# Two more units summed by the vector engine, and four squares of every sixteen on another queue

## The chip, the cores and the metric

The kernel runs on one core of a Trainium2 chip. A core has five engines that run their own instruction streams in order and wait for each other by semaphores: PE (TensorE, matmuls; PEld is its weight load), DVE (VectorE), ACT (ScalarE), POOL (GpSimd) and SP (SyncE, which here only issues DMAs). The metric is the device time in microseconds of one execution. Before the change it is 930.43 us, the median of three runs (929.61 to 931.49).

## The reference

Eight batches of twelve heads go through softmax attention with a soft cap on the scores; the result, 448 tokens by 768 channels per batch, goes through a mixing layer. Shapes: q, k, v are 8 x 12 x 448 x 64, all in fp32.

```python
scores = scale * np.matmul(q, k.transpose(0, 1, 3, 2))
scores = cap * np.tanh(scores / cap)
attn = np.exp(scores - max)                      # max over the last axis
x = (attn / (sum(attn) + 1e-9)) @ v              # then heads side by side: 448 x 768
theta = x @ w_theta
y = w_tok_r @ (x * np.cos(theta)) + w_tok_i @ (x * np.sin(theta))
u = x + y
out = u + np.maximum(u @ w_ch, 0.0)
```

## The kernel before

**Units and slots.** Two heads make a unit, so a batch has six units and the kernel 48. The main loop (L519) runs over slots s. Slot s computes the scores of unit s in two halves (A and B, L216; one PSUM tile holds a half, so B waits for the tanh of A) and the products of unit s-1 with v (V, L260). ACT does tanh (tA, tB, L221) and exp (eA, eB, L227), and copies the product out of PSUM (cV).

**Row sums.** The sum of the exponentials over the keys is taken on PE with a matrix of ones (R, L280). Units 0 to 9 (`DIRECT = 10`) are summed straight from the exponentials: units 0 to 5 two at a time, units 6 to 9 each by itself. From unit 10 on DVE first adds the four key blocks up into `ps` (aA, one addition, L249; aB, two, L252), and PE sums only `ps`, for a pair of units at once. I inverts the sums of a pair, spreads them by DMA into `bc`, and N (L315) multiplies x with them, two units at a time.

**The mixing layer.** Batch b's layer runs in the six slots after its attention, beside the next batch's attention. T is theta (18 matmuls for each of the six channel blocks), y two ACT steps out of PSUM, d three DVE steps of range reduction (L362 to L364), sc the cosine and sine of a pair of channel blocks on ACT (L369, L370), r the products with x (L374) and f a transpose of 32 x 32 squares (L378). D (`carry`, L380) then moves the squares of a pair of blocks to their places by 16 DMAs of 56 KB (L388). h and l split the result into high and low parts (ACT L393, DVE L399), M multiplies with the token weights (L408 to L410), m adds to x (L413), u splits u, C is the channel product (L334 to L336), c its output (L420), X the split of the next batch's x. P splits q and k of a coming unit on DVE (L192, L193; from unit 14 on).

**Weights.** Weights come as raw words and are split on the chip, one block at a time (`WEIGHTS`; `>` loads, `*` scales on ACT at L110, `#` scales on DVE at L113, a bare name does the rest). The splitting of th, tk and ch blocks fills the first eight slots and is finished in slots 8, 11, 12 and 13. The high part of a block is a copy, on DVE (L125), or on ACT (L123) where the block says so: ch3, ch4 and ch5.

**What sets the order.** No scheduler reorders anything: each engine gets its instructions in the order in which the scripts name them. `FRONT` stands for slots 0 to 7, `PARTS` for the six slots of each later batch, `OTHER` for slots that differ, such as (0, 0) and (0, 1), which are slots 8 and 9. A word's instructions stand behind all earlier words' on their engine, DMAs on the queue that issues them.

Of the kernel before, what the change touches and what calls it, by code (L numbers as in the profile page):

```python
# [19 lines left out]
P = 128  # L20
# [5 lines left out]

FIRST = 8

DIRECT = 10

FILL = {"before the branch": 8, "first scores": 2, "half": 8, "slot": 10}

# [4 lines left out]
def softcap_attn_then_spectral_mix(ctx, tc, qk2, v, cap, w_theta, w_tok, w_ch, outT):  # L37
    nc = tc.nc
    B, NP, P, _, S = qk2.shape
# [14 lines left out]
    w_theta, w_ch = (w.bitcast(I32).rearrange("m p j (n two) -> m p j n two", two=2) for w in (w_theta, w_ch))  # L54
# [16 lines left out]
    wch_h = const.tile([P, NJ, DM], F32R, name="wch_h")  # L71
    wch_l = const.tile([P, NJ, DM], F32R, name="wch_l")
# [56 lines left out]
    def room_g(at):  # L129
        def room():  # L130
            st = g_sb[:, at : at + 3 * DM]
            raw = st[:, : 2 * DM].rearrange("p (j n two) -> p j n two", j=NJ, two=2)
            return raw, st[:, 2 * DM :].rearrange("p (j n) -> p j n", j=NJ)
        return room

    def room_t(i, name):
        def room():
            raw = g_sb[:, (12 + 2 * i) * S : (14 + 2 * i) * S]
            t = wk.tile([P, S], F32, tag="zl", name=f"{name}_t", bufs=2)
            return raw.rearrange("p (n two) -> p n two", two=2), t  # L140
        return room

    steps = {}

    def weight_steps():
        for m in range(NJ):
            ms = slice(m * P, (m + 1) * P)
            steps["th", m] = Split(room_g((0, 6 * S)[m % 2]), w_theta[m], wth_h[:, :, ms], wth_l[:, :, ms])
            steps["ch", m] = Split(room_g((0, 6 * S, 8 * S, 0, 8 * S, 0)[m]), w_ch[m], wch_h[:, :, ms], wch_l[:, :, ms], m > 2)
        for c in range(NC2):  # L150
            steps["tk", c] = Split(room_t(c % 2, f"swk{c}"), w_tok[c], wtk_h[:, c], wtk_l[:, c])


    WEIGHTS = {
# [86 lines left out]
    def add_half(k, half):  # L241

        if k < DIRECT and not state["general"]:
            return
# [37 lines left out]
    def sums(k, halves=(0, 1)):  # L282

        alone = state["general"] or NP <= k < DIRECT
        if not alone and k % 2 == 0:
# [94 lines left out]
    def carry(b, i):  # L380

        at = 4 * S * i
        to = 4 * S * (i - 1) if i else 12 * S
        z, t = (g_sb[:, n : n + 4 * S].rearrange("p (c m d) -> p c m d", m=4, d=32) for n in (at, to))
        for m in range(4):
            for d in range(4):
                queue = nc.gpsimd if b == B - 1 and i and d % 2 else nc.sync
                queue.dma_start(t[32 * m : 32 * m + 32, :, d, :], z[32 * d : 32 * d + 32, :, m, :])  # L388

    def z_high(b, j, h):  # L390
# [27 lines left out]
    def chan_out(b, m):  # L418
# [4 lines left out]
    FRONT = "A tA w0 eA Va R0 B tB Vb cV v R1 q w1 n I eB aA aB w2 x"  # L423
    PARTS = (
# [8 lines left out]
    )  # L433
    OTHER = {
        (0, 0): "A tA eA V cV w0 v R I B tB eB aA aB q T0 y0 d0 w1 T1 y1 d1 sc0 w2 T2 y2 r0 r1 f0 f1 d2 D0",
        (0, 1): "A tA eA V cV N v R I B tB eB aA aB q T3 y3 d3 sc1 T4 r2 r3 f2 f3 D1 y4 d4 T5 y5 d5",
        (B - 2, 4): "V cV u3 u4 u5 R I C0 c0 C1 X0 X1 c1 C2 X2 X3 c2",
        (B - 2, 5): "N X4 X5 T0+ y0+ d0+ T1+ y1+ d1+ sc0+ T2+ r0+ r1+ f0+ f1+ D0+ y2+ d2+ T3+ y3+ d3+ sc1+ T4+ r2+ r3+ f2+ f3+ D1+ y4+ d4+"
                    " T5+ y5+ d5+ sc2+ C3 c3 r4+ h0a+ l0a+ h0b+ l0b+ r5+ f4+ f5+ D2+ C4 c4 h1a+ C5 c5",
# [4 lines left out]
    def pipeline(general):  # L444
# [6 lines left out]
        def run(s, b, word):  # L451
# [33 lines left out]
            elif word == "I":  # L485
                if done:
                    invert(k)
            elif word == "q":
                if s + 2 <= WHOLE:
                    load_qk(s + 2)  # L490
            elif word == "P":
                if WHOLE <= s + 1 < NS:
                    prep(s + 1)
            elif name == "w":
                weights(s, "abc"[i])
            elif word == "N":
                norm(s - 3)
                norm(s - 2)
            elif word == "n":
                for n in {4: (0, 1), 5: (2, 3), 7: (4, 5)}.get(s, ()):  # L500
                    norm(n)
            elif word == "x":
                for j in {5: range(2), 6: range(2, 4), 7: range(4, NJ)}.get(s, ()):
                    split_x(0, j, "xs")
            elif name == "u":
                split_x(b, i, "us")
            elif name == "X":
                if b + 1 < B:
                    split_x(b + 1, i, "xs")
            elif name in ("h", "l", "M"):  # L510
                {"h": z_high, "l": z_low, "M": mix}[name](b, i, half)
            else:
                {"T": theta, "y": turns, "d": reduce, "sc": sincos, "r": rotate, "f": flip, "D": carry, "m": mix_out, "C": chan,
                 "c": chan_out}[name](b, i)
# [12 lines left out]

    load_consts()
    weight_steps()
    load_qk(0)  # L530
    first = (("th", 0), ("th", 1))
# [46 lines left out]
```

## Time and profile before

| | |
|---|---|
| median of three runs | 930.43 us |
| profiled execution: its time, its span | 927.67 us, 925.9 us |
| PE busy | 912.4 us (99%) |
| DVE busy | 653.0 us (71%) |
| ACT busy | 613.8 us (66%) |
| POOL busy | 10.8 us (1%) |
| share of PE, ACT, DVE in the chain that ended last | 80%, 11%, 5% |
| granted clock of PE | full in all 40 slices |

Busy is the time in which an engine has an instruction running; the span goes from the first instruction to the last. The profiled execution lies below the three timed runs, so differences are to be taken from its own time and then set against the median. Slots differ in length: slot 8 runs from about 75.9 to 96.7 us, slot 9 from 96.7 to 117.6, and from slot 14 on a batch takes about 110 us.

### The profile page before, as it was taken

To read this page: it belongs to the slowest core of one execution; us is meant where nothing else is said; L and a number is where in the kernel's file an instruction comes from. 1 tells how busy PE (TensorE), PEld (TensorE's weight loads), DVE (VectorE), ACT (ScalarE), POOL (GpSimd) and SP (SyncE) were. 2 spreads that over 40 slices of the span, in tenths; PEclk is the share of its full clock that TensorE was granted. 3 is DMA by queue.
4 is the path that set the end of the run, shared out by engine and by line. 5 is a ranking of instruction groups with operands and counts; after the bars stand their busy time and mean duration, and the time that the engine had idled before them with its cause. 6 is when DMAs were issued, how large, how long until landed. Compare 5 with 4: busy or idle time off the path is not lost.

```text
span 925.9 us, 12930 instructions
## 1 busy us (share of the span) xinstructions
PE 912.4 (99%) x4912; PEld 661.1 (71%) x4912; DVE 653.0 (71%) x967; ACT 613.8 (66%) x639; POOL 10.8 (1%) x22
## 2 busy tenths in 40 slices
PE   8999999999999999999999999999999999999997
PEld 4334666578767777787687677867877777789986
DVE  5998766987865588656977568665786558865741
ACT  7997875568855697646975579646885569753420
POOL 0000000000000000000000000000000000000310
PEclk9999999999999999999999999999999999999999
DMA  6764155432533244232552226422253333411611
GB/s 231 241 202 137 27 120 151 138 98 58 120 75 107 83 82 94 72 113 60 100 126 75 70 63 123 95 80 85 58 120 77 101 89 79 77 41 38 113 36 62
DMA packets 201863, 90.67 MB, mean 98 GB/s; under 512 B 175296, under 2 KB 187584, under 8 KB 201792
## 3 DMA queue, kind: packets, MB, share of 16 engines
q1 hardware_dynamic: 201280, 88.84, 37.8%
q0 software_dynamic: 512, 0.92, 0.5%
q8 instruction: 40, 0.66, 0.3%
q14 instruction: 31, 0.25, 0.1%
HBM read 45.68 MB, written 11.01 MB: 61 GB/s over the span
## 4 chain that ended last, share of the span: by engine, by line
PE 80%; ACT 11%; DVE 5%; issue 1%; DMA 1%; SPq 1%; DVEq 0%; ACTq 0%
PE s L216 11%; PE a L260 11%; PE mx L410 7%; PE mx L408 7%; PE mx L409 7%; PE ch L334 6%; PE ch L336 6%; PE ch L335 6%; PE th L334 5%; PE th L335 5%; PE th L336 5%; ACT p L221 4%; PE r L280 4%; ACT L221 2%; ACT p L227 1%
## 5 line engine op out<-in xcount | busy, mean ns | idle before, releaser
L221 ACT ACTIVATE p<-s,qscale 112x1792 f32<-112x1792 f32 x96 | 168.5, 1755 | 118.9 <-PE s L216 117.1
L227 ACT ACTIVATE p<-p,cap_sb 112x1792 f32<-112x1792 f32 x96 | 170.3, 1787 | 0.3
L260 PE MATMUL a<-p,v 112*64 112x448 f32 x768 | 156.5, 546 | 0.0
L260 PEld LDWEIGHTS a<-p,v 112*64 112x64 f32 x768 | 50.2, 136 | 88.2 <-issue 77.0
L334 PE MATMUL th<-xs,wth_h 128*128 128x448 f32 x288 | 107.0, 372 | 0.0
L334 PE MATMUL ch<-us,wch_h 128*128 128x448 f32 x288 | 106.9, 371 | 0.0
L335 PE MATMUL ch<-us,wch_h 128*128 128x448 f32 x288 | 105.5, 366 | 0.0
L335 PE MATMUL th<-xs,wth_h 128*128 128x448 f32 x288 | 105.5, 366 | 0.0
L336 PE MATMUL ch<-us,wch_l 128*128 128x448 f32 x288 | 105.5, 366 | 0.0
L336 PE MATMUL th<-xs,wth_l 128*128 128x448 f32 x288 | 105.4, 366 | 0.0
L252 DVE TENSOR_TENSOR ps<-ps,p 112x896 f32<-112x896 f32 x76 | 82.8, 1089 | 2.2
L410 PE MATMUL mx<-wtk_h,zl_False 128*128 128x448 f32 x192 | 70.6, 367 | 1.9 <-DVE zl_False L399 1.3
L408 PE MATMUL mx<-wtk_h,zh_False 128*128 128x448 f32 x192 | 71.4, 372 | 0.0
L420 DVE SCALAR_TENSOR_TENSOR x<-ch,x 128x448 f32<-128x448 f32 x48 | 29.8, 622 | 58.6 <-PE ch L336 58.6
L409 PE MATMUL mx<-wtk_l,zh_False 128*128 128x448 f32 x192 | 70.1, 365 | 0.0
L374 DVE TENSOR_TENSOR g_sb<-g_sb,x 128x896 f32<-128x896 f32 x48 | 50.8, 1086 | 19.0 <-ACT g_sb L370 19.0
L362 DVE SCALAR_TENSOR_TENSOR g_sb<-g_sb 128x448 f32<-128x448 f32 x48 | 29.5, 615 | 46.7 <-ACT g_sb L357 46.7
L334 PEld LDWEIGHTS ch<-us,wch_h 128*128 128x128 f32 x288 | 54.1, 188 | 9.6 <-issue 4.6
L334 PEld LDWEIGHTS th<-xs,wth_h 128*128 128x128 f32 x288 | 54.1, 188 | 9.6 <-issue 4.5
L336 PEld LDWEIGHTS ch<-us,wch_l 128*128 128x128 f32 x288 | 54.1, 188 | 4.8 <-DVE wch_l L127 0.2
L335 PEld LDWEIGHTS ch<-us,wch_h 128*128 128x128 f32 x288 | 54.2, 188 | 4.6 <-DVE us L326 0.3
L335 PEld LDWEIGHTS th<-xs,wth_h 128*128 128x128 f32 x288 | 54.2, 188 | 4.6 <-DVE xs L326 0.3
(82 smaller groups left out, 1567.1 us busy)
## 6 DMA issues: line engine op xcount, KB each, us to landing
g_sb<-g_sb SPq DMA_DIRECT2D x368, 56.0 KB, 2.0
qk_sb<-in_qk SPq DMA_DIRECT2D x35, 448.0 KB, 3.6
v<-in_v SPq DMA_DIRECT2D x48, 224.0 KB, 2.8
bc<-ri SPq DMA_DIRECT2D x96, 112.0 KB, 2.3
out_dram<-x SPq DMA_DIRECT2D x48, 224.0 KB, 1.9
qk<-in_qk SPq DMA_DIRECT2D x13, 448.0 KB, 3.8
g_sb<-in_wth SPq DMA_DIRECT2D x6, 768.0 KB, 5.5
g_sb<-in_wch SPq DMA_DIRECT2D x6, 768.0 KB, 5.8
```

The source lines that it names most:

```text
L216: nc.tensor.matmul(sp[:CP, i, hh, :S], kk[k][rows, 1, ks], qq[k][rows, 0, :], start=n == 0, stop=n == len(products) - 1)
L221: nc.scalar.activation(pt[k, half], spt.pop((k, half))[:CP, :, :, :S], AF.Tanh, scale=qscale[:CP])
L227: nc.scalar.activation(pp, pp, AF.Exp, scale=cap_sb[:CP])
L252: nc.vector.tensor_tensor(pst[k], pst[k], pt[k, 1][:, i], op=ALU.add)
L260: nc.tensor.matmul(acc[hh * D : (hh + 1) * D, :S], va[:, hh, c, :], pt[k, c // 2][:, c % 2, hh, :], start=c == 0, stop=c == NCH - 1)
L334: nc.tensor.matmul(acc[:, :S], wh[:, j, ms], t[:, 0, :], start=j == 0, stop=False)
L335: nc.tensor.matmul(acc[:, :S], wh[:, j, ms], t[:, 1, :], start=False, stop=False)
L336: nc.tensor.matmul(acc[:, :S], wl[:, j, ms], t[:, 0, :], start=False, stop=j == NJ - 1)
L374: nc.vector.tensor_tensor(z, z, X[b, j].unsqueeze(1).broadcast_to([P, 2, S]), op=ALU.mult)
L408: nc.tensor.matmul(acc[:, :S], zh, wtk_h[:, c, :], start=c == 0, stop=False)
L409: nc.tensor.matmul(acc[:, :S], zh, wtk_l[:, c, :], start=False, stop=False)
L410: nc.tensor.matmul(acc[:, :S], zl, wtk_h[:, c, :], start=False, stop=c == NC2 - 1)
```

## The change

Five things are changed.

1. `DIRECT` is 8: units 8 and 9 are added up by DVE (six additions) and their sums taken together, by R of slot 10.
2. In slots 8 and 9 the first sines (sc0), the work behind them (r0, r1, f0, f1) and the squares D0 move from slot 8 to the front of slot 9; aB stands behind the next theta product.
3. N moves: in each batch's slot 1 it was the last word, and now stands in slot 2 behind the first mix (`N-` means the N of the slot before); in slot 13 it stands, with P, behind the split of channel block 5.
4. The scalings of th1 and tk0 go from ACT in slot 0 to DVE in slot 1, and the copy of ch4 from ACT to DVE.
5. Of the 16 squares of each pair the four with d = 3 are issued from GpSimd's queue, in every batch; in the last batch the first pair stays on SP, and the second and third pair put four on that queue instead of eight.

```diff
-DIRECT = 10
+DIRECT = 8
...
-            steps["ch", m] = Split(room_g(...), w_ch[m], wch_h[:, :, ms], wch_l[:, :, ms], m > 2)
+            steps["ch", m] = Split(room_g(...), w_ch[m], wch_h[:, :, ms], wch_l[:, :, ms], m in (3, 5))
...
-        (0, "a"): "#th0", (0, "b"): "th0 >th2", (0, "c"): "*th1 *tk0", (1, "b"): "tk0 >tk2 th1 >th3",
+        (0, "a"): "#th0", (0, "b"): "th0 >th2", (1, "b"): "#tk0 tk0 >tk2 #th1 th1 >th3",
...
-                queue = nc.gpsimd if b == B - 1 and i and d % 2 else nc.sync
+                queue = nc.gpsimd if (b < B - 1 or i) and d == 3 else nc.sync
...
+        (0, 5): "A tA V cV w0 v R I B tB q w1 N P eA C3 c3 aA eB C4 c4 aB w2 C5 X0 X1 X2 X3 X4 X5 c5",
-        (0, 0): "A tA eA V cV w0 v R I B tB eB aA aB q T0 y0 d0 w1 T1 y1 d1 sc0 w2 T2 y2 r0 r1 f0 f1 d2 D0",
-        (0, 1): "A tA eA V cV N v R I B tB eB aA aB q T3 y3 d3 sc1 T4 r2 r3 f2 f3 D1 y4 d4 T5 y5 d5",
+        (0, 0): "A tA eA V cV w0 v R I B tB eB aA q T0 aB y0 d0 w1 T1 y1 d1 w2 T2 y2 d2",
+        (0, 1): "A tA eA sc0 r0 r1 f0 f1 D0 V cV v R I B tB eB aA q T3 y3 d3 sc1 aB T4 r2 r3 f2 f3 D1 y4 d4 T5 y5 d5",
```

The first place is PE in slot 9, whose scores are of unit 9. `s` are scores, `a` the products of unit 8, `r` row sums, `p` exponentials, `th` theta. Before:

```order
L216 MATMUL s_0_778<-qk_593 112x448 x4
L260 MATMUL a_786<-p_0_612,v_587 64x448 x4
L260 MATMUL a_786<-p_1_660,v_587 64x448 x4
L280 MATMUL r_801<-p_0_612,ones_sb 32x448 x4
L280 MATMUL r_801<-p_1_660,ones_sb 32x448 x4
L216 MATMUL s_1_810<-qk_593 112x448 x4
L334 MATMUL th_3_820<-xs_0_467,wth_h 128x448
```

After, at the same place:

```order
L216 MATMUL s_0_760<-qk_593 112x448 x4
L260 MATMUL a_790<-p_0_612,v_587 64x448 x4
L260 MATMUL a_790<-p_1_660,v_587 64x448 x4
L216 MATMUL s_1_803<-qk_593 112x448 x4
L334 MATMUL th_3_815<-xs_0_467,wth_h 128x448
```

The two groups of sums of unit 8 are gone from here. In slot 10, where the sums of unit 9 stood in the same way, PE now has the sums of both units, from `ps`:

```order
L216 MATMUL s_0_911<-qk_669 112x448 x4
L260 MATMUL a_918<-p_0_761,v_638 64x448 x4
L260 MATMUL a_918<-p_1_804,v_638 64x448 x4
L280 MATMUL r_943<-ps_667,ones_sb 32x448 x2
L280 MATMUL r_943<-ps_811,ones_sb 32x448 x2
L216 MATMUL s_1_948<-qk_669 112x448 x4
L408 MATMUL mx_0_956<-wtk_h,zh_0_False 128x448
```

The second place is ACT at the turn from slot 12 to slot 13. L110 is the scaling of ch4, L123 the copy of its high part, L221 the tanh of unit 13's first half. Before:

```order
L227 ACTIVATE p_0_1233<-p_0_1233,cap_sb 112x1792
L227 ACTIVATE p_1_1276<-p_1_1276,cap_sb 112x1792
L110 ACTIVATE g_sb<-g_sb 128x768
L123 CAST wch_h<-g_sb 128x6x128
L221 ACTIVATE p_0_1370<-s_0_1369,qscale 112x1792
L267 COPY x_1387<-a_1378 128x448
```

After:

```order
L227 ACTIVATE p_0_1229<-p_0_1229,cap_sb 112x1792
L227 ACTIVATE p_1_1272<-p_1_1272,cap_sb 112x1792
L110 ACTIVATE g_sb<-g_sb 128x768
L221 ACTIVATE p_0_1366<-s_0_1365,qscale 112x1792
L267 COPY x_1381<-a_1372 128x448
L221 ACTIVATE p_1_1386<-s_1_1385,qscale 112x1792
```

The copy no longer stands between the scaling and the tanh. The third place is DVE at the first mix of batch 1 (the same in later batches): L315 is N, `zl` the low halves, L374 and L378 rotation and transpose of the third pair. Before:

```order
L364 TENSOR_SCALAR g_sb<-g_sb 128x448
L315 TENSOR_TENSOR x_1387<-bc_1533,x_1387 128x448
L315 TENSOR_TENSOR x_1519<-bc_1536,x_1519 128x448
L399 TENSOR_TENSOR zl_0_False<-g_sb,zh_0_False 128x512
L399 TENSOR_TENSOR zl_0_True<-g_sb,zh_0_True 128x384
L192 CAST hi_1868<-qk_sb 128x896
L193 TENSOR_TENSOR lo_1869<-qk_sb,hi_1868 128x896
L399 TENSOR_TENSOR zl_1_False<-g_sb,zh_1_False 128x512
L374 TENSOR_TENSOR g_sb<-g_sb,x_1107 128x896
L399 TENSOR_TENSOR zl_1_True<-g_sb,zh_1_True 128x384
```

After:

```order
L364 TENSOR_SCALAR g_sb<-g_sb 128x448
L399 TENSOR_TENSOR zl_0_False<-g_sb,zh_0_False 128x512
L399 TENSOR_TENSOR zl_0_True<-g_sb,zh_0_True 128x384
L192 CAST hi_1862<-qk_sb 128x896
L193 TENSOR_TENSOR lo_1863<-qk_sb,hi_1862 128x896
L399 TENSOR_TENSOR zl_1_False<-g_sb,zh_1_False 128x512
L374 TENSOR_TENSOR g_sb<-g_sb,x_1103 128x896
L399 TENSOR_TENSOR zl_1_True<-g_sb,zh_1_True 128x384
L315 TENSOR_TENSOR x_1381<-bc_1529,x_1381 128x448
L315 TENSOR_TENSOR x_1515<-bc_1532,x_1515 128x448
L374 TENSOR_TENSOR g_sb<-g_sb,x_1244 128x896
L378 STREAM_TRANSPOSE g_sb<-g_sb 128x896
```

The two rows of N have moved from before the first low halves to behind the second mix's, ahead of the last rotation.

## Rows read from the trace of the kernel before

**Rows 1.** The page's part 1: busy us, share of span, instructions of each engine.

```profile
PE 912.4 (99%) x4912; PEld 661.1 (71%) x4912; DVE 653.0 (71%) x967; ACT 613.8 (66%) x639; POOL 10.8 (1%) x22
```

**Rows 2.** Chain of waits, 60 to 260 us: start, us, instructions merged.

```profile
101.59 3.13 PE r L280 x16
...
122.47 3.13 PE r L280 x16
...
202.39 0.89 PE r L280 x8
```

**Rows 3.** Timeline, slots 0 and 1: start, us, instruction [idle before, releaser].

```profile
13.71 1.29 PE L216 MATMUL s<-qk 64*112 64x448 f32 x6
...
14.77 1.41 ACT L110 ACTIVATE g_sb<-g_sb 128x768 f32<-128x768 f32 x2
...
17.86 0.63 PE L216 MATMUL s<-qk 64*112 64x448 f32 x2 [1.20 <-ACT p L221]
```

**Rows 4.** Timeline, end of slot 12 and slot 13 (unit 13).

```profile
182.25 0.83 ACT L123 CAST wch_h<-g_sb 128x768 fp32r<-128x768 f32 x1 [4.09 <-DVE g_sb L119]
...
182.99 1.75 ACT L221 ACTIVATE p<-s,qscale 112x1792 f32<-112x1792 f32 x1
...
184.79 0.63 PE L216 MATMUL s<-qk 64*112 64x448 f32 x2 [1.58 <-ACT p L221]
```

**Rows 5.** Timeline, first mix of batch 2.

```profile
349.41 1.16 DVE L315 TENSOR_TENSOR x<-bc,x 128x448 f32<-128x448 f32 x2
...
350.48 0.69 DVE L399 TENSOR_TENSOR zl_False<-g_sb,zh_False 128x512 fp32r<-128x512 f32 x1
...
350.75 0.37 PE L409 MATMUL mx<-wtk_l,zh_False 128*128 128x448 f32 x1
...
351.23 0.47 PE L410 MATMUL mx<-wtk_h,zl_False 128*128 128x448 f32 x1
```

**Rows 6.** Timeline, last batch: GpSimd's queue, then the fifth mix.

```profile
863.70 0.89 POOL L388 DMA_DIRECT2D g_sb<-g_sb  x1 [862.81 <-DVE g_sb L362]
...
867.50 0.64 POOL L388 DMA_DIRECT2D g_sb<-g_sb  x1 [1.93 <-DMA g_sb<-g_sb]
...
883.81 1.34 POOL L388 DMA_DIRECT2D g_sb<-g_sb  x2 [0.96 <-issue]
...
887.43 0.62 ACT L393 CAST zh_False<-g_sb 128x512 fp32r<-128x512 f32 x1 [4.99 <-DMA g_sb<-g_sb]
...
890.08 0.47 PE L410 MATMUL mx<-wtk_h,zl_False 128*128 128x448 f32 x1 [1.30 <-DVE zl_False L399]
```

**Rows 7.** Groups by line and shape: count | busy, mean ns | idle.

```profile
L252 DVE TENSOR_TENSOR ps<-ps,p 112x896 f32<-112x896 f32 x76 | 82.8, 1089 | 2.2
```

**Rows 8.** Timeline of DVE, slot 8.

```profile
90.63 0.62 DVE L362 SCALAR_TENSOR_TENSOR g_sb<-g_sb 128x448 f32<-128x448 f32 x1 [3.63 <-ACT g_sb L357]
```

**Rows 9.** Busy us by stretch: PE, PEld, DVE, ACT, POOL; clock, DMA.

```profile
96.75:117.63 20.88, 20.88 (x104) 13.24 (x104) 16.26 (x24) 18.16 (x18) 0.00 (x0) 1.00 0.22 37
...
155.96:186.25 30.29, 28.71 (x145) 17.86 (x143) 29.67 (x43) 15.68 (x17) 0.00 (x0) 1.00 0.42 136
```

**Rows 10.** Timeline, head and end of DVE's long run, unit 14's scores.

```profile
155.48 0.56 DVE L399 TENSOR_TENSOR zl_True<-g_sb,zh_True 128x384 fp32r<-128x384 f32 x1 [1.11 <-PE mx L410]
...
193.30 0.96 DVE L127 TENSOR_TENSOR wch_l<-g_sb 128x768 fp32r<-128x768 f32 x1
...
197.77 0.46 PE L216 MATMUL s<-hi 64*112 64x448 f32 x2
```

**Rows 11.** Timeline, third mix and third pair's squares of batch 2.

```profile
357.91 0.65 DVE L399 TENSOR_TENSOR zl_False<-g_sb,zh_False 128x512 fp32r<-128x512 f32 x1
...
359.66 10.96 SPq L388 DMA_DIRECT2D g_sb<-g_sb  x16
...
359.74 0.36 PE L410 MATMUL mx<-wtk_h,zl_False 128*128 128x448 f32 x1
...
372.11 0.62 ACT L393 CAST zh_False<-g_sb 128x512 fp32r<-128x512 f32 x1 [0.57 <-DMA g_sb<-g_sb]
```

More of the change, by code (lines that the diff above doesn't have):

```diff
@@ L148, in weight_steps @@
             steps["th", m] = Split(room_g((0, 6 * S)[m % 2]), w_theta[m], wth_h[:, :, ms], wth_l[:, :, ms])
-            steps["ch", m] = Split(room_g((0, 6 * S, 8 * S, 0, 8 * S, 0)[m]), w_ch[m], wch_h[:, :, ms], wch_l[:, :, ms], m > 2)
+            steps["ch", m] = Split(room_g((0, 6 * S, 8 * S, 0, 8 * S, 0)[m]), w_ch[m], wch_h[:, :, ms], wch_l[:, :, ms], m in (3, 5))
         for c in range(NC2):
```

4 rows, old and new, of the table PARTS are left out of this document.

## The prediction

> **What bounds the kernel.** I read the page's first part, then the chain of waits, then the timeline wherever the chain left PE. The first part gives PE busy 912.4 of 925.9 us [rows 1], so all idle time of PE is 13.5 us. A step is worth something only if it takes matmuls off PE or closes one of PE's gaps; DVE and ACT count when they open a new one. The chain shows the first kind: the row sums of units 8 and 9 stand on it with 3.13 us each, sixteen matmuls apiece, while a pair that DVE has added up beforehand takes 0.89 [rows 2]. The timeline shows the second kind, in brackets or as a late start: 1.20 in the first slot, 1.58 in slot 13, a short one at the first mix of each batch, 1.30 in the last batch [rows 3 to 6].
>
> **The sums of units 8 and 9.** PE loses 3.13 + 3.13 and gains 0.89: 5.37 us, on the path since PE has no gap around either. DVE gets three additions per unit, 6 x 1.09 = 6.5 us [rows 7]. They are hidden if DVE has room: in slot 8 it stands 3.63 us before the first reduction [rows 8], where the first addition fits whole; the other two wait for the second exponential and push the reductions back by under 1 us, and nothing on PE reads these before slot 10. In slot 9 DVE is busy 16.26 of 20.88 us [rows 9]; the slot shrinks to 20.88 - 3.13 = 17.75 and receives two products, two transposes and three additions, which is why the normalization (N) and the first sines move. ACT is tighter: its 18.16 us in that stretch [rows 9] already hold the first sines, which now merely come later in it; against 17.75 it is 0.4 over. I charge nothing, because the first mix needs the squares of pair 0 only in slot 10, and keep 0.4 for the range. Without this cover, the scores of unit 10 would wait for the tanh before them.
>
> **Scalings of the first weights.** ACT scales two weight blocks between the exponential of unit 0 and the tanh of unit 1, 14.77 to 16.08 [rows 3]; then PE waits, and resumes at 17.86. After the change tanh waits for the scores alone, which end at 13.71 + 1.29 = 15.00; with 1.75 of tanh [rows 4] PE can resume at 16.8: 1.0 gained, and never more than the idle 1.20. DVE gets the two scalings where it waits for them today.
>
> **Channel block 4.** In slot 12 ACT's copy of this block waits 4.09 us for DVE, and queued behind it stands the tanh at 182.99, for which PE idles 1.58 [rows 4]. With the copy on DVE the tanh goes as soon as its scores are there, during the sixteen products of the unit before, so the gap closes: 1.58. DVE gets a copy, at most the 0.83 of ACT's [rows 4] (I take 0.55), inside a run in which it is busy 29.67 of 30.29 us [rows 9]. What is late next is the preparation of unit 14 (P), which now stands behind the split of block 5. Today P comes first and the split ends at 193.30 + 0.96 = 194.26, against scores of unit 14 at 197.77 [rows 10]. Reordered, P ends last, at 194.26 + 0.55 = 194.8. The run of DVE begins right behind a wait of 1.11 for PE's mixes at 155.48 [rows 10], and these come 5.37 + 1.0 = 6.4 earlier, so P ends at 188.4 and PE is there at 197.77 - 6.4 - 1.58 = 189.8. It holds, by 1.4.
>
> **Normalization moved past the first mix.** In each of batches 1 to 6 DVE runs N at 349.41 just before the low halves at 350.48; the second low product on PE should follow 350.75 by 0.20, as its neighbours do, and comes at 351.23: 0.28 late [rows 5]. Six batches: 1.7. Behind N now stand the last rotations and the low half of the third mix, which ends at 357.91 + 0.65 = 358.56 for a matmul at 359.74 [rows 11]; 1.07 of N uses 1.07 of this 1.18, so the wait may come back there. Bounds 0 and 2.3 (with the 0.1 that PE loses in restarting); I take 1.6, near the row.
>
> **Squares on GpSimd's queue.** SP issues 16 squares in 10.96 us [rows 11], 0.685 each; twelve take 8.2. This frees 2.7 us per pair, where today only ACT waits, 0.57 [rows 11], and PE does not: nothing gained in batches 0 to 6. The last batch is different. Its GpSimd queue carries sixteen squares, from 863.70 to 883.81 + 1.34 = 885.15 [rows 6], 1.34 each, eight of them of the last pair; then ACT's cast at 887.43 ends 4.99 of waiting for a DMA, and PE idles 1.30 at 890.08 [rows 6]. Afterwards the last pair puts four there (5.4 us) and twelve on SP (8.2), against 8 x 1.34 = 10.7 today: 2.5 earlier, more than the gap. Gain 1.3; bound 0 if SP comes late from the second pair, of which it now has twelve.
>
> The Trainium skill speaks against this edit: its page "SBUF — State Buffer", section "SBUF: two separate sides", says that a DMA from GpSimd's queue has its descriptors written by GpSimd, which is locked out of a shared port while DVE runs certain one-input operations; it gives 0.62 us for such a DMA alone and 3.1 beside a DVE copy. By that figure four squares would take 12.4 us, more than the 10.96 of all sixteen today. The trace agrees only faintly: the first issue takes 0.89, the later ones 0.63 to 0.67 [rows 6], with DVE at work beside them.
>
> **The sum.** 5.37 + 1.0 + 1.58 + 1.6 + 1.3 = 10.85, so 10.9 us less. The profiled execution has a span of 925.9 and took 927.67; less 10.9 that is 915.0 and 916.8. The runs that count have a median of 930.43, 2.8 above it; the same 10.9 off gives **919.5**. With every bound at its best (0.2 more in front, 0.7 in N) it is 11.8 less, 918.6; a median of three can stray by 1 (929.61 to 931.49). With N, the last batch and the 0.4 of ACT all lost it is 7.6 less, 922.8.
>
> **Rivals.**
> *A, DVE's long run does not move.* If DVE is late into the run from 155.96 on, because slots 8 to 10 left it a backlog, P still ends at 194.8 and unit 14's scores cannot come before: PE is 197.77 - 194.8 = 3.0 earlier there instead of 8.0. That costs 5.0: 924.5. For it: 29.67 busy of 30.29. Against: the wait of 1.11 at the head of the run, and the 3.63 us and more that DVE idles in slots 8 and 9.
> *B, slower: GpSimd's queue is the last to land.* The place is the third pair's squares of batches 0 to 6. A GpSimd issue waits until earlier ones have landed: the worst spacing seen is 1.93 idle plus 0.64 [rows 6], 2.57. Four at that pace take 10.3, and 11.1 with the 0.8 by which N delays them: even with today's 10.96. From 2.6 per square on, ACT's cast and the fourth mix come late. If each is also held for a DVE operation of 1.09 [rows 7], it is 3.66, four take 14.6, and the mix is 4.5 late. Halfway, 3.1 per square, it is 2.2 late in seven batches, 15.4; less the 10.9 gained: 935. Against: 1.34 was the mean over sixteen.
> *C, moved waits.* The gaps close and reopen next door: N's at the third mix, the sums' in ACT's overfull slot 9, while A takes half its price. What is left is 5.37 + 1.0 less 4 to 6: about no change, 929.5.
>
> **How the numbers follow.** Forecast 0.71, A 0.15, B 0.08, C 0.06. 0.2% of the median is 1.9 us, about what can be told from no change: forecast and A are faster, C is mostly the same, B slower. That gives 0.87, 0.05, 0.08. The range reaches from 917.0 (918.6 less the straying of a median, with a little for PE restarts that I did not count) to 926.0 (A and its straying); it leaves out B, C and the ends, 0.2 in all.
>
> **What would show it.** Right: on the chain no sums of sixteen in slots 9 and 10; slot 9 some 17.8 long; PE resumes at 16.8 in slot 1; no ACT copy of block 4 and no idle before unit 13's second scores; the first low product of each mix 0.20 behind its neighbour; no PE gap in the last batch's fifth mix; GpSimd's four squares landing before SP's twelve. Wrong: PE idle before unit 14's scores with DVE's P just ended (A); ACT's cast for the fifth mix waiting for a GpSimd square, and PE's mixes behind it, in every batch (B); PE waiting for a low half in the third mix (C).

## The result, and the profile after

The changed kernel takes 919.68 us (919.0 to 920.27, five runs) against 930.43, a ratio of 0.9885 with an interval from 0.9871 to 0.9900. Forecast were 919.5. The total came out; that the parts do not stand side by side, as the sum had them, only the experiments showed.

The profiled execution of the changed kernel took 920.27, with a span of 918.1. Page, part 1, against [rows 1]:

```profile
PE 908.1 (99%) x4888; PEld 660.3 (72%) x4888; DVE 660.6 (72%) x976; ACT 612.7 (67%) x636; POOL 59.1 (6%) x98
```

PE has 24 matmuls fewer (32 sums gone, 8 added) and 10.0 us of idle time instead of 13.5. The view of PE's waits names it (engine, line, releaser: us in all, times, longest). First the kernel before, then the changed one:

```profile
PE s L216 <- ACT p L221: 4.0, 8, 1.6
PE mx L410 <- DVE zl_False L399: 1.3, 1, 1.3
```

```profile
PE s L216 <- ACT p L221: 1.2, 6, 0.2
...
PE mx L410 <- DVE zl_False L399: 0.9, 1, 0.9
```

Two waits for a tanh are gone (1.20, of which 0.21 is left, and 1.58), and so is the last batch's for a low half. But there is again one wait for a low half, and it is a new one, in batch 0. The timeline of PE after (start, us, instruction, idle before it) at the places of [rows 3], of this new wait, and of [rows 4], [rows 5] and [rows 6]:

```profile
19.59 0.63 PE L216 MATMUL s<-qk 64*112 64x448 f32 x2 [0.21 <-ACT p L221]
...
125.25 0.47 PE L410 MATMUL mx<-wtk_h,zl_False 128*128 128x448 f32 x1 [0.87 <-DVE zl_False L399]
...
180.80 1.76 PE L216 MATMUL s<-qk 64*112 64x448 f32 x8
...
346.33 0.36 PE L409 MATMUL mx<-wtk_l,zh_False 128*128 128x448 f32 x1
346.53 0.37 PE L410 MATMUL mx<-wtk_h,zl_False 128*128 128x448 f32 x1
```

Slot 13's scores follow without a gap, and the first low product of batch 2 stands 0.20 behind its neighbour. The chain of waits after (start, us, what) shows [rows 2] and where the new wait comes from:

```profile
98.50 1.72 PE s L216 x8
100.23 1.78 ACT p L221
102.06 1.79 issue
103.85 1.28 ACT L369
105.14 1.05 ACT g_sb L369
...
108.76 1.77 ACT p L221
...
114.90 1.01 DVE ps L252
115.94 1.09 DVE ps L252
117.03 2.00 DVE g_sb L374 x2
119.03 2.02 DVE g_sb L378 x2
121.11 3.39 DMA g_sb<-g_sb
124.50 0.70 DVE zl_False L399
...
162.12 0.89 PE r L280 x8
```

The sums of sixteen are gone from slots 9 and 10. For the first time the chain runs through slot 9 on ACT and DVE: it leaves PE at the scores of unit 9 and returns at the low half of the first mix (the row named `issue` is ACT's exponential). Its DMA step, at 121.11, is inferred and is not what held the low half: it is a square of the second pair, while the sixteen squares that this half needs had all landed by 121.24. Ahead of the low half DVE runs the transposes and then the two range reductions d4 and d5, to 123.94.

**Step by step.** I set the start of every matmul of one trace against the same matmul of the other; a step is where their distance changes.

| place (us, before) | step | forecast |
|---|---|---|
| first scores, 5.4 to 9.5 | +2.72 | none |
| scalings, 17.86 | -0.99 | -1.0 |
| sums, 104.66 and 125.53 | -3.11, -2.14 | -5.37 |
| first mix of batch 0, 127.74 | +1.14 | none |
| block 4, 184.79 | -1.61 | -1.58 |
| N, first mixes of batches 1 to 6 | -1.78 | -1.6 |
| last batch, 888.10 and 890.08 | -2.03 | -1.3 |
| sum | -7.80 | -10.85 |

The first row has nothing to do with the change. PE in the first 10 us, before and after:

```profile
5.37 0.57 PE L86 MATMUL fill<-ones_sb 112*32 112x112 f32 x4 [1.23 <-DVE qscale L63]
5.87 1.76 PE L216 MATMUL s<-qk_sb 64*112 64x448 f32 x8
```

```profile
5.66 0.95 PE L86 MATMUL fill<-ones_sb 112*32 112x112 f32 x4 [1.51 <-DVE qscale L63]
6.53 3.33 PE L216 MATMUL s<-qk_sb 64*112 64x448 f32 x8
```

The same eight matmuls take 1.76 and 3.33. In 14 profiles of 12 kernels, alike up to there, the first scores of the second half start anywhere between 9.48 and 12.43; the profile of before was the earliest of all, that of after is among the latest. It is the clock: the trace's record of the granted clock begins with a rise to 1.00 at 4.17 in the one and at 11.36 in the other. Ahead of that rise there is no entry, and a view prints 1.00 there, as does the row of full clock in the table of before; but PE's fill matmuls (L86) start every 0.19 up to the rise and every 0.10 behind it. The Trainium skill, page "TensorE: Matmul & The Clock Gate", section "What's actually happening", says that the number of slow matmuls with which a program begins differs from run to run; the 14 profiles agree, by up to 2.9 us. Without this row the traces differ by 10.5, the medians by 10.75.

### The profile page after: what moved, and what is told of

Its sections match the earlier page's. It is cut to its first block, busy times and chain, and to the rows that moved or that the text cites. A ratio compares the mean times of both kernels' runs of the same rounds, so it can differ in the third digit from the quotient of the medians.

```text
span 918.1 us, 13077 instructions
## 1 busy us (share of the span) xinstructions
PE 908.1 (99%) x4888; PEld 660.3 (72%) x4888; DVE 660.6 (72%) x976; ACT 612.7 (67%) x636; POOL 59.1 (6%) x98
## 4 chain that ended last, share of the span: by engine, by line
PE 95%; ACT 2%; DVE 1%; DMA 1%; issue 1%; SPq 0%
PE s L216 15%; PE a L260 15%; PE mx L408 8%; PE mx L409 7%; PE mx L410 7%; PE ch L334 7%; PE ch L335 6%; PE ch L336 6%; PE th L334 6%; PE th L335 6%; PE th L336 6%; PE r L280 4%; ACT p L221 2%; PE fill L86 1%; DMA cap_sb<-in_cap 0%
## 5 line engine op out<-in xcount | busy, mean ns | idle before, releaser
L221 ACT ACTIVATE p<-s,qscale 112x1792 f32<-112x1792 f32 x96 | 168.6, 1757 | 124.0 <-PE s L216 122.3
L388 POOL DMA_DIRECT2D g_sb<-g_sb x92 | 58.7, 639 | 813.0 <-ACT g_sb L357 382.0
L252 DVE TENSOR_TENSOR ps<-ps,p 112x896 f32<-112x896 f32 x80 | 87.1, 1089 | 3.5 <-ACT p L227 1.3
L374 DVE TENSOR_TENSOR g_sb<-g_sb,x 128x896 f32<-128x896 f32 x48 | 50.8, 1086 | 17.5 <-ACT g_sb L370 17.5
L334 PEld LDWEIGHTS ch<-us,wch_h 128*128 128x128 f32 x288 | 54.1, 188 | 9.7 <-issue 4.6
L334 PEld LDWEIGHTS th<-xs,wth_h 128*128 128x128 f32 x288 | 54.1, 188 | 9.6 <-issue 4.5
L362 DVE SCALAR_TENSOR_TENSOR g_sb<-g_sb 128x448 f32<-128x448 f32 x48 | 29.4, 613 | 39.7 <-ACT g_sb L357 39.7
L336 PEld LDWEIGHTS th<-xs,wth_l 128*128 128x128 f32 x288 | 54.1, 188 | 4.7
```

The source lines that it names most:

```text
L221: nc.scalar.activation(pt[k, half], spt.pop((k, half))[:CP, :, :, :S], AF.Tanh, scale=qscale[:CP])
L252: nc.vector.tensor_tensor(pst[k], pst[k], pt[k, 1][:, i], op=ALU.add)
L334: nc.tensor.matmul(acc[:, :S], wh[:, j, ms], t[:, 0, :], start=j == 0, stop=False)
L336: nc.tensor.matmul(acc[:, :S], wl[:, j, ms], t[:, 0, :], start=False, stop=j == NJ - 1)
```

## The experiments

Each kernel was timed in five rounds beside the kernel before, four kernels on a chip. Differences below are between medians, also of different groups; before had 929.8, 930.54 and 930.16 in the three groups of four and 930.43 beside the changed kernel, so such a difference is uncertain by some 0.7. Steps in traces do not depend on it.

| kernel | us | ratio to before, interval |
|---|---|---|
| changed, sums back | 922.6 | 0.9928 (0.9914 to 0.9941) |
| changed, d5 behind the low half | 918.06 | 0.9879 (0.9863 to 0.9895) |
| changed, N back | 921.68 | 0.9909 (0.9889 to 0.9928) |
| changed, squares back | 928.6 | 0.9991 (0.9978 to 1.0004) |
| before, sums alone | 932.3 | 1.0009 (0.9996 to 1.0022) |
| before, quarter alone | 928.65 | 0.9970 (0.9959 to 0.9981) |
| changed, sums and squares back | 928.91 | 0.9977 (0.9967 to 0.9987) |
| changed, half on GpSimd | 939.63 | 1.0087 (1.0071 to 1.0102) |
| before, sums and quarter | 923.95 | 0.9927 (0.9913 to 0.9941) |
| before, N alone | 930.57 | 1.0004 (0.9991 to 1.0017) |
| changed, again | 919.08 | 0.9872 (0.9855 to 0.9890) |
| d5 behind the low half, again | 917.73 | 0.9864 (0.9846 to 0.9882) |

**Sums back.**

```diff
-DIRECT = 8
+DIRECT = 10
...
+        (0, 0): "A tA eA V cV w0 v R I B tB eB aA aB q T0 y0 d0 w1 T1 y1 d1 sc0 w2 T2 y2 r0 r1 f0 f1 d2 D0",
+        (0, 1): "A tA eA V cV v R I B tB eB aA aB q T3 y3 d3 sc1 T4 r2 r3 f2 f3 D1 y4 d4 T5 y5 d5",
```

> The changed kernel, but with DIRECT = 10 again and the words of slots 8 and 9 (batch 0, parts 0 and 1) in the old order, N staying where the change put it. Theory: the sums are worth 5.25 us on PE (3.11 in slot 9, 2.14 in slot 10), but 1.14 of it is given back at batch 0's first mix, where PE waits for a low half because ACT and DVE are late out of slot 9; so this kernel is 4.1 slower than the changed one, 923.8, and its PE has no gap at batch 0's first mix. Rival 1: the gap of 1.14 has nothing to do with the sums (it comes with N or with the second queue of the squares): then the gap stays and this kernel is 5.25 slower, 924.9. Rival 2: the whole gain of the sums lies here and the other parts are worth nothing: 930.

2.9 slower than the changed kernel; in the trace +3.11 and +2.14 at the old places and -1.03 at batch 0's first mix. The gap comes with the sums. (Of these 4.2 the trace gives back 0.8 later, 0.12 at a time.)

**The last range reduction behind the first low half.** It is a move on DVE alone: d5 goes from the end of slot 9 into slot 10.

```diff
+        (0, 1): "A tA eA sc0 r0 r1 f0 f1 D0 V cV v R I B tB eB aA q T3 y3 d3 sc1 aB T4 r2 r3 f2 f3 D1 y4 d4 T5 y5",
+        (0, 2): "A tA V h0a l0a d5 h0b l0b h1a cV sc2 w0 v R B q P w1 M0a l1a h1b tB r4 M0b l1b N- r5 f4 h2a M1a l2a f5 D2 eA M1b h2b l2b I m0 M2a h3a"
+        " eB m1 aA M2b m2 w2",
```

> The changed kernel, but DVE's last range reduction of batch 0 (d5, three instructions, 1.45 us) moves from the end of slot 9 to behind the first low half of slot 10. Theory: DVE's order alone makes PE wait 1.03 (and 0.1 in restarting) at batch 0's first mix, since the low half stands behind 1.45 of work that nobody needs yet; with d5 behind it the low half is there 1.45 earlier, the gap goes, and the kernel is 1.1 faster than the changed one: 918.5. Rival 1: what holds the low half is the landing of a square or DVE's run through its semaphores (0.56 of idle before it), which stays: gain 0.5 or less, 919.2. Rival 2: d5 comes late for the sines behind it and a later mix waits instead: no gain, 919.7 or more, with a new gap between 128 and 140 us.

918.06, and in the trace the step of -1.06 is at the low product and nothing comes behind it. DVE in the second run of this kernel (timeline; L364 ends d4, L362 begins d5), where PE's product follows at 123.04 without a wait:

```profile
120.83 0.55 DVE L364 TENSOR_SCALAR g_sb<-g_sb 128x448 int32<-128x448 int32 x1
121.78 0.69 DVE L399 TENSOR_TENSOR zl_False<-g_sb,zh_False 128x512 fp32r<-128x512 f32 x1 [0.40 <-ACT zh_True L393]
122.39 0.62 DVE L362 SCALAR_TENSOR_TENSOR g_sb<-g_sb 128x448 f32<-128x448 f32 x1
```

The idle of 0.40 before the low half stays, as rival 1 said, but 1.45 of work behind it was enough.

**N back** in batches 1 to 6 (`d5 N w2` in part 1, no `N-` in part 2).

> The changed kernel, but in batches 1 to 6 N stands again at the end of part 1, ahead of the first mix; batch 0 and slot 13 stay as changed. Theory: the move is worth what the offset between the two traces shows, 0.25 to 0.39 per batch, 1.8 over six: 921.5, and PE's first low product of each of the six first mixes comes 0.27 late again, with 0.1 lost behind it. Rival: the offset comes from somewhere else (the low halves were late because of the squares' queue or of DVE's backlog), N is worth nothing: 919.7, no late product.

2.0 slower in the medians; in the trace 0.25 to 0.27 at each of the six first low products, with the small losses behind them 2.4 in all. The term was 1.6.

**Squares back.**

```diff
-                queue = nc.gpsimd if (b < B - 1 or i) and d == 3 else nc.sync
+                queue = nc.gpsimd if b == B - 1 and i and d % 2 else nc.sync
```

> The changed kernel, but the squares go as before: all on SP in batches 0 to 6, and in the last batch eight of sixteen of the second and third pair on GpSimd's queue. Theory: the queue matters in the last batch alone, where it closed a gap of 1.30 with its restarts, 2.0 in all: 921.7, the gap again before the fifth mix of the last batch, and no PE start moved by more than 0.1 us in batches 1 to 6. Rival 1: the quarter on GpSimd relieved SP in batches 0 to 6 too (part of the 1.8 that I put down to N): then 922 to 923.5, with late low products in batches 1 to 6. Rival 2: the quarter costs something in batches 0 to 6, and the gap of 1.14 at batch 0's first mix is part of it (the low half waits for four more semaphores): then that gap shrinks by 0.2 to 0.6 and the kernel takes 921.2.

8.9 slower instead of 2: the largest surprise, and more than rival 1 allowed. SP, ACT and PE at batch 0's third mix (timeline), the first that reads the second pair's squares, and the stretches behind it (busy us of PE, PEld, DVE, ACT, POOL, then the granted clock). The expectations call it the second mix; the fifth mix of a batch, the first that reads the third pair, they and rival B call the fourth:

```profile
122.27 10.84 SPq L388 DMA_DIRECT2D g_sb<-g_sb  x16
...
134.69 0.62 ACT L393 CAST zh_False<-g_sb 128x512 fp32r<-128x512 f32 x1 [3.30 <-DMA g_sb<-g_sb]
...
135.36 0.74 PE L408 MATMUL mx<-wtk_h,zh_False 128*128 128x448 f32 x1 [2.94 <-ACT zh_False L393]
135.90 0.58 PE L409 MATMUL mx<-wtk_l,zh_False 128*128 128x448 f32 x1
136.27 0.58 PE L410 MATMUL mx<-wtk_h,zl_False 128*128 128x448 f32 x1
```

```profile
135.90:138.00 2.10, 2.10 (x7) 1.76 (x6) 1.72 (x4) 2.10 (x4) 0.00 (x0) 0.50 0.38 150
138.00:140.00 2.00, 2.00 (x10) 1.84 (x10) 1.93 (x5) 1.62 (x1) 0.00 (x0) 0.93 0.49 82
```

SP takes up these sixteen squares 2.5 later than in the kernel before (122.27 less 0.36 of later start, against 119.45), while PE comes 5.2 earlier. PE waits 1.05 at the first mix and 2.94 at the third, and from 134.9, late in this wait, to 138.3 the granted clock is 0.50, the lower level: matmuls every 0.37 instead of 0.20, 1.3 more. Another 2.1 are late third pairs in batches 1 to 6 (steps of 0.2 to 1.2 at the fifth mixes of three of them), 2.2 the last batch.

**The sums alone, on the kernel before** (`DIRECT`, slots 8 and 9, and N of units 6 and 7 as in the change, nothing else).

> The kernel before with the first part of the change alone: DIRECT = 8 and the new words of slots 8 and 9 (and, since N of units 6 and 7 leaves slot 9 with them, N behind batch 0's first mix). All squares of batches 0 to 6 stay on SP. Theory: PE gains 5.25 on the sums, but the squares of batch 0 go out later while PE comes earlier, and as in the kernel with the squares put back PE waits about 1.05 at batch 0's first mix and 2.9 at its second, with some 1.3 more at half clock behind the second wait: 5.3 lost, so no gain that can be told: 930 against 929.8 before. Rival: the parts add up, the sums are worth what they were worth in the whole change, 3 to 4.1: 925.7 to 926.8.

932.3, no gain. In the trace -3.13 and -2.16 for the sums, then +1.64 at batch 0's first mix and +4.7 at its third. That leaves +1.1; the last batch of this execution (933.95, the second slowest of twelve) loses 2.6 more, of which more below, under N alone.

**The quarter alone, on the kernel before.**

> The kernel before with the fifth part alone: a quarter of the squares on GpSimd's queue. Theory: with the old sums no mix of batches 0 to 6 waits long for squares, so the quarter is worth the last batch alone (1.30 of idle with its restarts, 2.0) and at most 0.2 more: 927.7 against 929.8. Rival 1: it relieves SP in every batch, whatever the sums do, and is worth the 8.9 that its removal cost the changed kernel: 921. Rival 2: what it gives in the last batch it takes in the others (four more semaphores before the first low half): 929.8.

1.9 faster; in the trace -2.0 in the last batch, and no step above 0.15 in batches 0 to 6. The small steps there add up to 0.7 the other way, so rival 2 has a little truth.

**Sums and squares back.** The squares cost 8.9 behind the new sums; behind the old ones:

> The changed kernel with the sums and the words of slots 8 and 9 put back, and the squares put back too. Putting the sums back alone gave 922.6, the squares alone 928.6, the changed kernel 919.7. Theory: 4.5 to 5 of the 8.9 that the squares cost lie in batch 0 and hang on the sums (squares issued later while PE is earlier); with the sums back they vanish, and what remains is 2.0 in the last batch and about 2 of late third-pair squares in batches 1 to 6: 926.6, hence both back is faster than the squares back alone. Rival: the two add up: 922.6 + 8.9 = 931.5.

928.91, so 6.3. The first mixes of batch 0 are quiet, as expected; but batches 1 to 6 lose 3.8, where I had expected 2, and the last batch 2.8. Both theory and rival missed it by some 2.5; that the two parts lean on each other holds (6.3 against 8.9), but a good part of the rest leans on something else than the sums.

**Half of the squares on GpSimd** (`d % 2` instead of `d == 3`).

> The changed kernel, but half of the squares of a pair (d odd, eight of sixteen) on GpSimd's queue instead of a quarter. Theory: that queue takes about 1.34 us per square however many there are, so eight take 10.7, as long as SP takes for all sixteen, and what the quarter gained is lost again where it mattered: batch 0's second mix waits 1 to 2.5 (with the clock), the third pair's squares of later batches come late by about 2 in all, and the last batch has its gap of 1.3 to 2.0 again: 924 to 926. Rival 1: the queue keeps more in flight when it has more to do and a square takes its 0.64 of issue: no change, 919.7. Rival 2: a square on that queue takes 3 us while DVE works beside it: eight take 24, each pair comes 13 late in eight batches, and the time is far above 950.

939.63, far outside. The price of a square was as expected, not what it does. All issues of these squares (least, median, longest ns), in the changed kernel, then with half:

```profile
L388 POOL DMA_DIRECT2D g_sb<-g_sb x92: 632/634/747, 111.9 to 872.0; - x92
```

```profile
L388 POOL DMA_DIRECT2D g_sb<-g_sb x184: 632/634/1100, 110.8 to 896.0; - x184
```

With half, one square starts every 1.3 to 1.7 and the eight of a pair take 11.2 to 15.1 to land, 2.8 to 8.4 later than SP's. PE waits for the high part, at nine mixes:

```profile
PE mx L408 <- ACT zh_False L393: 11.6, 9, 3.5
```

I had allowed 2 for all batches from 1 on, and nothing there for the half clock. It follows the two longest waits, 2.88 in batch 0 and 3.53 in batch 3 (13 matmuls of the mixes at 0.37 instead of 0.20), and none of the others, up to 1.76.

What sets the price of a square can be read from the landings. In all 14 traces GpSimd's queue never has more than two squares under way, where SP has up to eight. In the changed kernel 46 squares are the third or fourth of their four, and 45 of them start 0.30 or 0.31 us after the landing of the square two before them (issued at 859.38, landed at 861.58, the third starts at 861.89). With a median landing of 2.3 us this makes about 1.3 per square in the long run, and any square that lands late delays those behind it.

**Sums and quarter, on the kernel before.**

> The kernel before with two parts of the change: the sums of units 8 and 9 with the new words of slots 8 and 9 (and N of units 6 and 7 behind batch 0's first mix), and the quarter of the squares on GpSimd's queue. Alone, the first was worth nothing (932.3 against 930.5) and the second 1.9. Theory: the quarter takes away the waits of 4.4 to 5.5 that the sums bring in batch 0, so that the two together are worth 5.25 less the gap of 1.14 at the first mix, and 2.0 in the last batch: 6.1, or 924.4 against 930.5. Rival: the waits in batch 0 come from the other parts (ACT's scalings, N) and stay: the parts add up as they did alone, 929 to 930. By the theory the step from here to the kernel with N put back (921.7) is what the two ACT parts are worth, 1.0 and 1.6.

6.2 faster, where alone one was worth nothing and the other 1.9. The trace of N back, set against this one, has beside the start only two steps above 0.16, -0.99 at the scalings and -1.66 at block 4: the two ACT parts. Between the medians it is 2.3. (Each of the two was not undone by itself.)

**N alone, on the kernel before.**

> The kernel before with one part: N of batches 1 to 6 behind the first mix (slot 13 and batch 0 as before), all squares of these batches on SP. Theory: the first low product of six batches is no longer late, 2.3 gained, but N now delays the last rotation and with it the third pair's squares by 1.1, and with sixteen of them on SP the fourth mix waits, about 3.4 over the six batches (what the two kernels with the squares put back lost there: 2.2 and 3.4); net 0 to 1.5 slower: 930.5 to 932. Rival: the squares of the third pair have room for N's 1.1, and the move is worth its 2.3 without the quarter: 928.2.

930.57, no gain. Each first low product comes 0.25 to 0.27 earlier, and third pairs come late. Batch 4 (ACT, PE, SP's queue):

```profile
595.99 0.62 ACT L393 CAST zh_False<-g_sb 128x512 fp32r<-128x512 f32 x1 [2.56 <-DMA g_sb<-g_sb]
...
596.66 0.47 PE L408 MATMUL mx<-wtk_h,zh_False 128*128 128x448 f32 x1 [0.62 <-ACT zh_False L393]
```

```profile
582.56 11.68 SPq L388 DMA_DIRECT2D g_sb<-g_sb  x16
```

Up to the last batch the sum over six batches is +1.4. This execution took 935.23, the slowest of eleven, and its last batch loses another 4.1: PE waits 1.24 and 1.31 at the fifth mix, and then come 6.8 us at the lower clock, 2.8 more. Over the whole span its granted clock is 0.995, that of eight of the eleven 0.999 or more. The stretch, as above:

```profile
894.10:900.90 6.80, 6.22 (x17) 5.60 (x18) 2.85 (x5) 1.08 (x2) 0.00 (x0) 0.50 0.01 2
```

The sums alone show the same: waits of 0.81 and 1.31, then 0.50 from 895.5 to 899.0. With 0.93 and 1.31, in the kernel with sums and squares back, the clock stayed at 1.00. The kernel before has 1.30 alone. The first wait of each pair comes from GpSimd's queue: in these three kernels one of the last eight squares takes 3.5 to 4.0 to land, against 3.3 at most before, so the last square goes out 0.7 to 1.0 later beside PE, and ACT's cast waits for it.

**The changed kernel and the better one on one chip.**

> The changed kernel itself, for a comparison with the next one on the same chip: 919.7, the gap of 1.03 at batch 0's first mix again; the moment at which PE's matmuls go from half to full speed lies anywhere between 5.4 and 11.9 us, as in the ten profiles so far.

> The kernel with d5 behind the first low half of slot 10, again, beside the changed kernel. Theory: 1.1 faster than the changed one in the same call (0.12%), no gap at batch 0's first mix. Rival: the 1.6 between their medians so far was the start of PE's clock and chance; then the two medians agree within 0.5.

919.08 and 917.73. The intervals of the ratios overlap; the traces do not leave it open: -1.07 at the same low product, and no other step but the start. In both pairs of medians (1.6 and 1.35 apart, the first pair from different groups) the version with d5 behind the low half is the faster one.

## Why the prediction came out, point by point

**The total.** That it came out to 0.2 us is in part luck. The sums gave 4.1 after their gap instead of 5.4, the last batch 2.0 instead of 1.3, and both errors nearly cancel. More than that: without the quarter on GpSimd's queue the other four parts, forecast at 9.55, are worth 1.2 (929.8 less 928.6). The prediction had no term for this; that the quarter was in the same change saved its sum.

**The sums.** The price was right (5.25 for 5.37); "hidden if DVE has room" was not. The step that failed is ACT's slot 9: I took 18.16 us busy of 20.88 [rows 9] as fitting into 17.75 but for 0.4. ACT's rows after:

```profile
98.53 0.54 ACT L356 ACTIVATE g_sb<-th 128x448 f32<-128x448 f32 x1 [2.52 <-PE th L336]
...
100.23 1.77 ACT L221 ACTIVATE p<-s,qscale 112x1792 f32<-112x1792 f32 x1 [0.55 <-PE s L216]
...
120.21 1.75 ACT L221 ACTIVATE p<-s,qscale 112x1792 f32<-112x1792 f32 x1
```

It waits 2.52 and 0.55 ahead of the slot's tanh, where the sines used to run, and from 100.23 on it is busy without a gap above 0.25 to 121.96. The work did fit, but behind that tanh it ended no sooner than before: with 1.73 of later start taken off, the second sines end at 115.1 (114.91 before) and d5 on DVE, which has two additions more, at 122.2 (121.80), while PE comes 5.2 earlier. The first low half ends at 125.19 for a product due at 124.2. Cost 1.14. The experiment with the sums back shows that the gap comes with them, the one with d5 that DVE's order alone closes it. That both ACT's late sines and DVE's two additions, which end at 117.02, hold the second rotation (116.94) is read from the rows and was not tested apart.

**Scalings, block 4, N.** 0.99, 1.61 and 1.8, or 2.4 by undoing it, for 1.0, 1.58 and 1.6. P of unit 14 held, by less than I wrote: it ends at 193.01 with PE there at 193.71, 0.7 instead of 1.4. The order was the reason: N and P used to stand between the last channel output and the split of block 5, and covered all but 0.20 of that split's wait for ACT's scaling. Now DVE waits there (timeline after):

```profile
185.20 0.56 DVE L118 TENSOR_SCALAR g_sb<-g_sb 128x768 int32<-128x768 int32 x1 [0.76 <-ACT g_sb L110]
```

The third mix held by a hair: its low half ends at 354.88 for a matmul at 355.02.

**The quarter.** The last batch was mis-sized (2.0 for 1.3: the gap carried 0.7 of late starts around it). The step that was wrong is "nothing gained in batches 0 to 6". On the kernel before it holds (quarter alone: no step above 0.15). But the sums bring PE earlier to batch 0's mixes and send its squares out later, N sends every third pair out 1.1 later, and what the quarter takes off a pair covers both. SP's share of batch 2's third pair after, 2.9 shorter than in [rows 11]:

```profile
355.96 8.06 SPq L388 DMA_DIRECT2D g_sb<-g_sb  x12
```

I had computed N's delay for rival B only, and the sums' not at all. So the change was worth its sum, and the parts were not: sums 0 alone and 4.3 beside the quarter (6.2 less 1.9), N 0 alone and 2.0 beside it, the quarter 1.9 alone and 8.9 beside the rest.

**The rivals.** A did not happen: DVE's run moved with PE, and P of unit 14 ended before PE needed it. B: that an issue on GpSimd's queue waits for earlier landings is so, but its conclusion is refuted for a quarter. SP's twelve landed last in all 23 pairs, by 1.6 to 4.2. The page "SBUF — State Buffer" of the Trainium skill (section "SBUF: two separate sides") would have had 3.1 us per such DMA beside a DVE copy; no issue in the rows above took more than 0.75, with DVE busy 72% of the time, and 1.10 with half on that queue. From issue to landing it was 2.0 to 4.2, median 2.3, in the changed kernel, and no run sets a square beside a copy alone. What B says of a queue that lands last, that the mixes behind it wait, is what the half showed: 20 us. C came true in one place, slot 9, for 1.14.

**From the profile to the median.** I took the 2.8 between the profiled execution and the median as a constant. The table's first row, 2.72, is an early start of the profiled execution of before, which is none of its timed runs. The other 13 profiled executions are timed runs of their kernels too: in twelve the second half starts between 10.84 and 12.43, 1.4 to 2.9 later than there, and the one early one (9.57, d5 behind the low half) is the fastest of its four, by 1.1. So a late start is the usual one, and it accounts for half or more of the 2.8. How the timed runs of before started is not on record.

## What to carry to other kernels

A cost put at nothing needs its cover named, and the cover has to be looked for among the other parts of the same change too: undoing one part of five cost 8.9 where that part alone gives 1.9. A busy share below a stretch's length does not say that the work fits behind the instruction that it now follows; look where in the stretch the engine's idle time lies. A PE that waits 3 us pays again afterwards, here 1.3 at half clock, and two waits of about 1.3 close together cost up to 2.8 more, so just-in-time transfers should be priced with the clock behind them. A queue that keeps few transfers under way is paced by their landings and not by their issues: count what is under way before giving it more.

## What the runs showed of the hardware

The granted clock was 0.50 for 3.4 us after, or from within, single waits of PE of 2.88, 2.93, 2.94 and 3.53 us, and for 3.4 and 6.8 us after pairs of waits 0.7 us apart (0.81 and 1.31, 1.24 and 1.31). After single waits of up to 1.76, and after two such pairs (0.44 and 1.30, 0.93 and 1.31), it stayed at 1.00. The first rise to 1.00 comes between 4.17 and 11.83 in the 14 traces, and the start of the second half of the first scores varies by 2.9 with it, between executions of the same instructions.

On the mean of a pair, a GpSimd queue with four squares starts one every 1.1 to 1.7 us, with eight one every 1.3 to 1.7, though an issue takes 0.63; SP starts one every 0.67. GpSimd's idle time is mostly named "issue" in the views; in all 14 traces it has at most two squares under way, and the next starts 0.3 us or more after a landing. What sets this limit of two, and why the same square lands in 2.0 us at one place and in 4.0 at another, stays open.
